# Two-piece weight splitting and a parametric rectifier, each with fewer operations

## The chip, the cores and the metric

The kernel runs on one core of a Trainium2 chip. Its engines are TensorE (PE for matmuls, PEld for the loads of their stationary operands), VectorE (DVE), ScalarE (ACT), GpSimd (POOL) and SyncE (SP), which issues transfers. The metric is the device time of one execution in microseconds, lower is better. The time before is the median of three runs, 837.42 us (836.5 to 838.45).

## The reference

The first half is attention inside chunks of 64 positions, for 8 batches, 8 heads, 576 positions and a head size of 64. Its result, laid out as 4608 tokens of 512 features, goes through a two-layer network with a parametric rectifier between the layers:

```python
scores = scale * np.matmul(q_c, k_c.transpose(0, 1, 2, 4, 3))
scores = scores - np.max(scores, axis=-1, keepdims=True)
attn = np.exp(scores)
attn = attn / (np.sum(attn, axis=-1, keepdims=True) + 1e-09)
out = np.matmul(attn, v_c)
...
h = x @ w_in                                   # 4608x512 by 512x2048
g = np.maximum(h, 0.0) + alpha * np.minimum(h, 0.0)
return (g @ w_out).astype(np.float32)          # 4608x2048 by 2048x512
```

The weights w_in and w_out arrive as 64-bit floats, all else as 32-bit floats. alpha has one value for each of the 2048 hidden features.

## The kernel before

**Precision.** TensorE runs the network's matmuls on the type fp32r. Every operand is held as two pieces, a rounded high piece and the rest, and each product is made of three passes: high by high, high by low, low by high.

**Splitting the weights.** The weights come as 32 raw tiles of 128x512 64-bit words (16 of w_in, 16 of w_out; 512 KB each), fetched by SP into a ring of three buffers (`raw` twice, `more` once). `split_weight` (lines 118 to 139) turns one raw tile into a high and a low piece by integer operations on the two 32-bit words of each float. ACT takes the absolute value (L130) and later copies the high piece with rounding (L134). DVE does the rest: limits of the exponent (L131), shift (L132), sign (L133), the low mantissa bits out of both words (L135, L136), the bare power of two (L137) and the product that is the low piece (L138). The tile `t1` carries the high part, `t3` the low bits.

**The rectifier.** `prelu` (L303 to L306) is called with a 128x512 block h in PSUM (or, in places, in SBUF), features on partitions. ACT makes relu(-h) (L304), ACT multiplies it by alpha per partition (L305), and DVE computes max(h, 0) minus that (L306). Then ACT rounds g to its high piece (L326) and DVE subtracts it for the low one (L327).

**Stages.** The first 1536 tokens (three blocks of 512) go through the network plainly: 48 steps, each of 12 matmuls for one slice of 128 hidden features (L314), the rectifier, and 12 matmuls into four PSUM accumulators (L339). The other 3072 tokens go in three pairs of blocks, by a product with seven block multiplications instead of eight (first layer L626, second layer L759), whose weight combinations are made ahead: `combine` adds and splits quarters of the weights (L523 to L540) in steps 20 to 43, and POOL stores them to memory (L501).

**Attention beside it.** Attention comes in 36 pieces of 128 tokens. The first eight run with scores (L180), maximum and its scaling (DVE L210, L212), eight exponentials (ACT L217), normalization (DVE L219 to L221), transposition on TensorE (L245), copies into a block-diagonal tile (ACT L252, L253), values (L263) and the split of x (ACT L295, DVE L296). The first four of these must be done before the first matmul of the network. The other 28 are "visits" between the steps: scores (L194), softmax, a DVE transposition (L228), eight small transfers (L235, tile `pT`), and values one visit later (L275), whose result ACT copies out (L291, L300; DVE L301).

**The order.** A scheduler with a model of the engines writes the order of each engine's instructions. Calls under `tc.high_priority` are moved forward. From step 20 on, TensorE's order is held to the order in the source (`pinned`); before that the scheduler is free with TensorE too. Each engine then runs its list strictly in order, so an instruction that waits holds back all behind it.

The per-partition factors alpha are fetched by a POOL transfer (L450) after POOL's memsets.

Of the kernel before, what the change touches and what calls it, by code (L numbers as in the profile page):

```python
# [9 lines left out]
F32 = mybir.dt.float32  # L10
F32R = mybir.dt.float32r
AF = mybir.ActivationFunctionType
ALU = mybir.AluOpType
AX = mybir.AxisListType
U32 = mybir.dt.uint32
# [3 lines left out]
def bits(pattern):  # L19
    return struct.unpack("f", struct.pack("I", pattern))[0]  # L20
# [7 lines left out]
def tile_local_attention_prelu_ffn(  # L28
# [12 lines left out]
    nc = tc.nc  # L41
    P = 128
# [5 lines left out]
    NF = w_in.shape[1]  # L48
# [13 lines left out]
    const = ctx.enter_context(tc.tile_pool(name="const", bufs=1))  # L62
# [4 lines left out]
    stage = ctx.enter_context(tc.tile_pool(name="stage", bufs=2))  # L67
# [5 lines left out]
    def f32(t):  # L73
        return t.bitcast(F32)
# [24 lines left out]
    ident = const.tile([P, P], F32, name="ident")  # L99
    make_identity(nc, ident)  # L100
    alpha_sb = const.tile([P, NF], F32, name="alpha_sb")

    pinned = [False]

# [9 lines left out]
    def fetch(side, f):  # L114
        name = ("raw", "raw", "more")[fetched[0] % 3]
        fetched[0] += 1
        raws[side, f] = stage.tile([P, 512], I64, name=name, bufs=2 if name == "raw" else 1)
        nc.sync.dma_start(out=raws[side, f], in_=(w_in if side == "wi" else w_out)[:, f])

    def split_weight(side, f):  # L120
        if (side, f) not in raws:
            fetch(side, f)
        raw = raws.pop((side, f))
        words = raw.bitcast(U32).rearrange("p (n two) -> p two n", two=2)
        low, high = words[:, 0], words[:, 1]
        t1 = stage.tile([P, 512], U32, name="t1")
        t3 = stage.tile([P, 512], U32, name="t3", bufs=1)
        w = const.tile([P, 2, 512], F32R, name=f"{side}{f}")
        hi, lo = w[:, 0], w[:, 1]
        nc.scalar.activation(f32(t1), f32(high), AF.Abs)  # L130
        nc.vector.tensor_scalar(f32(t1), f32(t1), bits(0x38000000), bits(0x47EFFFFF), op0=ALU.max, op1=ALU.min)  # L131
        nc.vector.tensor_scalar(t1, t1, 3, 0x3FFFF000, op0=ALU.logical_shift_left, op1=ALU.bitwise_and)  # L132
        nc.vector.scalar_tensor_tensor(t1, in0=high, scalar=0xC0000000, in1=t1, op0=ALU.bitwise_and, op1=ALU.bitwise_or)  # L133
        nc.scalar.copy(hi, f32(t1))  # L134
        nc.vector.tensor_scalar(t3, high, 0x1FF, 15, op0=ALU.bitwise_and, op1=ALU.logical_shift_left)  # L135
        nc.vector.scalar_tensor_tensor(t3, in0=low, scalar=17, in1=t3, op0=ALU.logical_shift_right, op1=ALU.bitwise_or)  # L136
        nc.vector.tensor_scalar(t1, t1, 0xFF800000, None, op0=ALU.bitwise_and)  # L137
        nc.vector.scalar_tensor_tensor(lo, in0=t3, scalar=2.0 ** -35, in1=f32(t1), op0=ALU.mult, op1=ALU.mult)  # L138
        return w

    def prepare(f, behind=None):
        with tc.issue_after(behind.ins) if behind else nullcontext():
            wi[f] = split_weight("wi", f)
            wo[f] = split_weight("wo", f)
# [157 lines left out]

    def prelu(g, h, f):  # L303
        nc.scalar.activation(g, h, AF.Relu, scale=-1.0)  # L304
        nc.scalar.activation(g, g, AF.Copy, scale=alpha_sb[:, f:f + 1])  # L305
        nc.vector.scalar_tensor_tensor(g, in0=h, scalar=0.0, in1=g, op0=ALU.max, op1=ALU.subtract)  # L306

    def ffn_in(x, f):
        xh, xl = x
        hps = ps_h.tile([P, TB], F32, name="ps_h")  # L310
        passes = [(0, xh), (0, xl), (1, xh)]
        for i, (l, xx) in enumerate(passes):
            for k in range(NK):
                pe(nc.tensor.matmul(  # L314
                    hps,
                    lhsT=wi[f][:, l, k * P:(k + 1) * P],
                    rhs=xx[:, k],
                    start=(i == 0 and k == 0),
                    stop=(i == 2 and k == NK - 1),
                ))  # L320
        g = gp.tile([P, TB], F32, name="g")
        gh = gp.tile([P, TB], F32R, name="gh")
        gl = gp.tile([P, TB], F32R, name="gl")
        with tc.high_priority(offset=HIGH):
            prelu(g, hps, f)
            nc.scalar.copy(gh, g)  # L326
            low = nc.vector.tensor_tensor(gl, g, f32(gh), op=ALU.subtract)  # L327
        stages["split"] = stages.get("split", [])[-1:] + [low]
        return gh, gl
# [118 lines left out]
    first_v(2)  # L448
    fetch("wi", 1)
    nc.gpsimd.dma_start(out=alpha_sb, in_=alpha)  # L450
    prepare(0)
    ready = 1
    for i in range(SPB + 2):
# [177 lines left out]
    def first_product(ops, g, j):  # L631
# [20 lines left out]
        with tc.high_priority(offset=HIGH):  # L652
            prelu(g[JF + j][:, 1], t, JF + j)
        for ps, i, f, col in ((c, 3, j, 1), (d, 4, JF + j, 0)):
            part(ps, i, False)
            with tc.high_priority(offset=HIGH):
                h = gp.tile([P, TB], F32, name="gl")
                nc.vector.tensor_tensor(h, ps, u, op=ALU.add)
                prelu(g[f][:, col], h, f)
# [199 lines left out]
    for pair in range(NPAIR):  # L859
# [4 lines left out]
        g = {}  # L864
# [49 lines left out]
```

## Time and profile before

| What | Value |
| --- | --- |
| Median of three runs | 837.42 us (836.5 to 838.45) |
| Span of the profiled execution, first to last instruction | 833.9 us |
| The runs above that span | 2.6 to 4.6 us, the median 3.5 us |
| PE busy | 804.0 us (96%) |
| DVE busy | 669.6 us (80%) |
| ACT busy | 548.0 us (66%) |
| Start of the first network matmul | 36.76 us |

The profile gives the profiled execution its span and no other time; the time of a run also holds what lies before the first and after the last instruction. In the lists, "idle before" is how long an engine stood still ahead of an instruction, with the one that released it behind the arrow. A matmul's shown duration is longer than the distance between two matmuls in a row, since they are pipelined.

### The profile page before, as it was taken

What the parts mean: (1) busy time and instruction counts of PE and PEld (TensorE: products, weight loads), DVE (VectorE), ACT (ScalarE), POOL (GpSimd) and SP (SyncE); (2) the same over time, 40 slices, a digit from 0 to 9 for tenths busy, and PEclk for the clock granted to TensorE, in tenths of its full rate; (3) what the DMA queues carried; (4) which work ended last, traced back from release to release, by engine and by line L of the source; (5) the groups of instructions that cost most, each with busy time, mean ns of one, the idle gap of its engine ahead of it and who ended that gap; (6) DMA issues with size and microseconds to landing.
All of it is one profiled execution on the core that took longest, in us unless ns stands there. A gap on an engine that the chain in (4) does not pass through costs nothing.

```text
span 833.9 us, 15382 instructions
## 1 busy us (share of the span) xinstructions
PE 804.0 (96%) x5248; PEld 642.6 (77%) x5248; DVE 669.6 (80%) x1240; ACT 548.0 (66%) x1420; POOL 215.4 (26%) x340
## 2 busy tenths in 40 slices
PE   4799999999999999999999999999999999999998
PEld 3577888777777778778778787787887888888886
DVE  6899999987788886677779996777789965668875
ACT  5986676657666776677886555777665546566452
POOL 4006223224244431111112242111122412121232
PEclk9999999999999999999999999999999999999999
DMA  9629778657698768688876799886557995555788
GB/s 287 206 77 344 236 243 266 199 162 209 200 254 216 247 211 262 214 258 270 263 240 209 225 252 329 256 274 199 192 196 242 244 300 184 188 191 187 235 230 231
DMA packets 73966, 192.40 MB, mean 231 GB/s; under 512 B 11664, under 2 KB 19104, under 8 KB 73760
## 3 DMA queue, kind: packets, MB, share of 16 engines
q0 software_dynamic: 38272, 127.43, 49.1%
q1 hardware_dynamic: 27248, 48.91, 18.5%
q10 hardware_dynamic: 8368, 15.08, 5.7%
q8 instruction: 42, 0.69, 0.3%
q14 instruction: 36, 0.29, 0.1%
HBM read 135.27 MB, written 42.99 MB: 214 GB/s over the span
## 4 chain that ended last, share of the span: by engine, by line
PE 73%; DVE 8%; DMA 7%; ACT 6%; SPq 3%; issue 3%; ACTq 0%; DVEq 0%; POOL 0%
PE ps_o L626 17%; PE ps_o L759 14%; PE ps_h L759 12%; PE ps_h L314 9%; PE ps_o L339 9%; PE ps_h L626 8%; SPq L235 3%; DMA v_sb<-v 2%; DMA pT<-t 2%; PE ps_a L275 1%; ACT pr L217 1%; DMA wi<-kT 1%; PE ps_a L194 1%; ACT wo L217 1%; DVE gl L327 1%
## 5 line engine op out<-in xcount | busy, mean ns | idle before, releaser
L339 PE MATMUL ps_o<-wo,gh 128*128 128x512 f32 x384 | 114.5, 396 | 0.6 <-ACT more L369 0.6
L314 PE MATMUL ps_h<-xh,wi 128*128 128x512 f32 x384 | 107.0, 401 | 1.8 <-DVE g L306 1.7
L314 PEld LDWEIGHTS ps_h<-xh,wi 128*128 128x128 f32 x384 | 71.8, 190 | 20.1 <-DVE g L306 2.6
L339 PEld LDWEIGHTS ps_o<-wo,gh 128*128 128x128 f32 x384 | 71.6, 188 | 18.1 <-ACT more L369 1.0
L339 PE MATMUL ps_o<-wo,gl 128*128 128x512 f32 x192 | 69.3, 396 | 0.4 <-DVE gl L327 0.4
L626 PE MATMUL ps_o<-wi,raw 128*128 128x512 f32 x171 | 67.9, 397 | 0.0
L217 ACT ACTIVATE pr<-ps_a,mx 128x64 f32<-128x64 f32 x224 | 67.4, 327 | 0.6
L626 PE MATMUL ps_o<-wo,raw 128*128 128x512 f32 x171 | 67.8, 396 | 0.0
L314 PE MATMUL ps_h<-xl,wi 128*128 128x512 f32 x192 | 52.6, 395 | 0.0
L326 ACT CAST gh<-g 128x512 fp32r<-128x512 f32 x48 | 29.8, 621 | 29.3 <-DVE g L306 27.4
L217 ACT ACTIVATION_READ_ACCUMULATOR pr<-ps_a,mx 128x1 f32 x224 | 48.9, 218 | 0.0
L564 POOL DMA_DIRECT2D raw<-wi_a x42 | 22.4, 535 | 102.1 <-PE ps_o L626 61.7
L304 ACT ACTIVATE wo<-gh 128x512 f32<-128x512 f32 x24 | 15.2, 634 | 51.1 <-DVE gh L649 51.1
L582 ACT CAST gh<-wi 128x512 fp32r<-128x512 f32 x45 | 28.0, 623 | 25.2 <-PE ps_o L759 10.9
L564 POOL DMA_DIRECT2D raw<-wo_a x42 | 22.4, 534 | 84.7 <-PE ps_o L759 43.9
L339 PEld LDWEIGHTS ps_o<-wo,gl 128*128 128x128 f32 x192 | 35.9, 188 | 9.6 <-DVE gl L327 0.8
L314 PEld LDWEIGHTS ps_h<-xl,wi 128*128 128x128 f32 x192 | 36.0, 188 | 8.5
L304 ACT ACTIVATE g<-ps_h 128x512 f32<-128x512 f32 x48 | 29.3, 611 | 18.3 <-PE ps_h L314 16.9
L626 PE MATMUL ps_o<-wi,wo 128*128 128x512 f32 x99 | 39.3, 397 | 0.0
L626 PE MATMUL ps_o<-wo,wo 128*128 128x512 f32 x99 | 39.1, 395 | 0.0
L626 PEld LDWEIGHTS ps_o<-wo,raw 128*128 128x128 f32 x171 | 32.2, 188 | 7.7
L626 PEld LDWEIGHTS ps_o<-wi,raw 128*128 128x128 f32 x171 | 32.1, 188 | 7.6
(252 smaller groups left out, 2280.9 us busy)
## 6 DMA issues: line engine op xcount, KB each, us to landing
raw<-wi_a POOLq DMA_DIRECT2D x42, 512.0 KB, 4.8
raw<-wo_a POOLq DMA_DIRECT2D x42, 512.0 KB, 4.1
wi<-wi_a POOLq DMA_DIRECT2D x21, 512.0 KB, 4.5
wo<-wi_a POOLq DMA_DIRECT2D x21, 512.0 KB, 4.8
wi<-wo_a POOLq DMA_DIRECT2D x21, 512.0 KB, 3.8
wo<-wo_a POOLq DMA_DIRECT2D x21, 512.0 KB, 4.3
v_sb<-v SPq DMA_DIRECT2D x28, 256.0 KB, 4.5
pT<-t SPq DMA_DIRECT2D x224, 32.0 KB, 3.9
```

The source lines that it names most:

```text
L194: pe(nc.tensor.matmul(att[par][c * C:(c + 1) * C, (NP + hp) * C:(NP + hp + 1) * C], lhsT=q_sb[rows, 2 * hp + c], rhs=kb[rows, 2 * hp + c], ...
L217: last = nc.scalar.activation(pr[:, g], one, AF.Exp, bias=mx[:, g], scale=SCALE, accum_out=sm[:, g])
L235: nc.sync.dma_start(out=pT[dst, i].rearrange("p h t -> p (h t)"), in_=tb[src, j].rearrange("p h t -> p (h t)"),)
L275: pe(nc.tensor.matmul(att[c][par * C:(par + 1) * C, hp * C:(hp + 1) * C], lhsT=v_sb[rows, h * C:(h + 1) * C], rhs=p[rows, :, par * NP + hp ...
L304: nc.scalar.activation(g, h, AF.Relu, scale=-1.0)
L314: pe(nc.tensor.matmul(hps, lhsT=wi[f][:, l, k * P:(k + 1) * P], rhs=xx[:, k], start=(i == 0 and k == 0), stop=(i == 2 and k == NK - 1),))
L326: nc.scalar.copy(gh, g)
L339: pe(nc.tensor.matmul(o, lhsT=a[:, ts], rhs=wo[f][:, l], start=(f == first and i == 0), stop=(f == last and i == 2),))
L564: streamed[0] = nc.gpsimd.dma_start(out=f32(t), in_=units[side][n])
L582: hi = nc.scalar.copy(t_hi, t)
L626: pe(nc.tensor.matmul(ps, lhsT=w[:, l, k * P:(k + 1) * P], rhs=xx[:, xl], start=first and at == 0, stop=at == n - 1, skip_group_check=not ...
L759: pe(nc.tensor.matmul(ps[m], lhsT=w[:, l, m * P:(m + 1) * P], rhs=xx, start=i != 6 and j == 0 and n == 0, stop=j == JF - 1 and n == 2, ski ...
```

## The change

The diff has two parts.

In `split_weight` the first word's mantissa is no longer cut after 11 bits: with the top three bits of the low word put behind it, `t1` becomes one 32-bit float with the weight's 24 leading bits. ACT rounds it to the high piece as before, and DVE subtracts the high piece from it for the low one. The three operations on `t3`, the mask and the multiplication go; one shift-and-or and one subtraction come. The low piece holds what 24 bits leave of the weight, where it held more bits before.

In `prelu` the sum is written as h + (1 - alpha) * relu(-h). A tile `rise` holds 1 - alpha, made once by DVE after alpha has come. ACT's multiplication by alpha goes; DVE's one operation multiplies by `rise` per partition and adds h.

```diff
@@ -99,6 +99,7 @@
     alpha_sb = const.tile([P, NF], F32, name="alpha_sb")
+    rise = const.tile([P, NF], F32, name="rise")
@@ -124,18 +125,15 @@
         t1 = stage.tile([P, 512], U32, name="t1")
-        t3 = stage.tile([P, 512], U32, name="t3", bufs=1)
         w = const.tile([P, 2, 512], F32R, name=f"{side}{f}")
         hi, lo = w[:, 0], w[:, 1]
         nc.scalar.activation(f32(t1), f32(high), AF.Abs)
         nc.vector.tensor_scalar(f32(t1), f32(t1), bits(0x38000000), bits(0x47EFFFFF), op0=ALU.max, op1=ALU.min)
-        nc.vector.tensor_scalar(t1, t1, 3, 0x3FFFF000, op0=ALU.logical_shift_left, op1=ALU.bitwise_and)
+        nc.vector.tensor_scalar(t1, t1, 3, 0x3FFFFFF8, op0=ALU.logical_shift_left, op1=ALU.bitwise_and)
         nc.vector.scalar_tensor_tensor(t1, in0=high, scalar=0xC0000000, in1=t1, op0=ALU.bitwise_and, op1=ALU.bitwise_or)
+        nc.vector.scalar_tensor_tensor(t1, in0=low, scalar=29, in1=t1, op0=ALU.logical_shift_right, op1=ALU.bitwise_or)
         nc.scalar.copy(hi, f32(t1))
-        nc.vector.tensor_scalar(t3, high, 0x1FF, 15, op0=ALU.bitwise_and, op1=ALU.logical_shift_left)
-        nc.vector.scalar_tensor_tensor(t3, in0=low, scalar=17, in1=t3, op0=ALU.logical_shift_right, op1=ALU.bitwise_or)
-        nc.vector.tensor_scalar(t1, t1, 0xFF800000, None, op0=ALU.bitwise_and)
-        nc.vector.scalar_tensor_tensor(lo, in0=t3, scalar=2.0 ** -35, in1=f32(t1), op0=ALU.mult, op1=ALU.mult)
+        nc.vector.tensor_tensor(lo, f32(t1), f32(hi), op=ALU.subtract)
         return w
@@ -302,8 +300,7 @@
     def prelu(g, h, f):
         nc.scalar.activation(g, h, AF.Relu, scale=-1.0)
-        nc.scalar.activation(g, g, AF.Copy, scale=alpha_sb[:, f:f + 1])
-        nc.vector.scalar_tensor_tensor(g, in0=h, scalar=0.0, in1=g, op0=ALU.max, op1=ALU.subtract)
+        nc.vector.scalar_tensor_tensor(g, in0=g, scalar=rise[:, f:f + 1], in1=h, op0=ALU.mult, op1=ALU.add)
@@ -448,6 +445,7 @@
     nc.gpsimd.dma_start(out=alpha_sb, in_=alpha)
+    nc.vector.tensor_scalar(rise, alpha_sb, -1.0, 1.0, op0=ALU.mult, op1=ALU.add)
     prepare(0)
```

The scheduler writes new orders from this. Line numbers below the two functions shift by 2 or 3 in the changed kernel: the new bits are L134, the subtraction L136, `rise` L448, the rectifier L302 and L303, g's rounding L323.

**DVE, the opening.** Names: `mx` and `sm` are a softmax's maximum and sum, `wo_94` the probabilities of the first two attention pieces. Before, from the first piece's maximum to its normalization:

```order
L210 TENSOR_REDUCE mx<-ps_a 128x8
L212 TENSOR_SCALAR mx<-mx 128x8
L137 TENSOR_SCALAR t_147<-t_147 128x512
L138 SCALAR_TENSOR_TENSOR wi_149<-t_148,t_147 128x512
L210 TENSOR_REDUCE mx<-ps_a 128x8
L219 TENSOR_SCALAR sm<-sm 128x8
L212 TENSOR_SCALAR mx<-mx 128x8
L220 RECIPROCAL sm<-sm 128x8
L221 TENSOR_TENSOR wo_94<-wo_94,sm 128x512
```

and in the changed kernel:

```order
L208 TENSOR_REDUCE mx<-ps_a 128x8
L134 SCALAR_TENSOR_TENSOR t_149<-raw,t_149 128x512
L210 TENSOR_SCALAR mx<-mx 128x8
L136 TENSOR_TENSOR wi_150<-t_149,wi_150 128x512
L208 TENSOR_REDUCE mx<-ps_a 128x8
L210 TENSOR_SCALAR mx<-mx 128x8
L217 TENSOR_SCALAR sm<-sm 128x8
L448 TENSOR_SCALAR rise<-alpha_sb 128x16
L218 RECIPROCAL sm<-sm 128x8
L219 TENSOR_TENSOR wo_94<-wo_94,sm 128x512
L208 TENSOR_REDUCE mx<-ps_a 128x8
```

`rise`, which waits for alpha, stands ahead of the first piece's reciprocal and normalization and of the third piece's maximum.

**PE, ahead of the network's first matmuls.** L180 are scores, L245 transpositions, L263 values of an attention piece, L314 the network (in the changed kernel L178, L243, L261, L311). Before:

```order
L180 MATMUL ps_a<-wo_86,wi_93 64x128 x8
L245 MATMUL ps_o_431<-ident,wo_94 128x128 x4
L263 MATMUL ps_o_334<-wi_91,wi_97 64x128 x8
L263 MATMUL ps_o_462<-wo_88,wo_96 64x128 x8
L314 MATMUL ps_h<-xh,wi_149 128x512 x4
L314 MATMUL ps_h<-xh,wi_506 128x512 x4
L245 MATMUL ps_o_473<-ident,wo_94 128x128 x4
L314 MATMUL ps_h<-xl,wi_149 128x512 x4
```

and in the changed kernel:

```order
L261 MATMUL ps_o_330<-wi_91,wi_97 64x128 x8
L178 MATMUL ps_a<-wo_86,wi_93 64x128 x8
L243 MATMUL ps_o_427<-ident,wo_94 128x128 x4
L311 MATMUL ps_h<-xh,wi_150 128x512 x4
L311 MATMUL ps_h<-xh,wi_501 128x512 x4
L243 MATMUL ps_o_469<-ident,wo_94 128x128 x4
L261 MATMUL ps_o_458<-wo_88,wo_96 64x128 x8
L311 MATMUL ps_h<-xl,wi_150 128x512 x4
```

The values of the fifth piece (on `wo_88`) stood ahead of the network's first matmuls and now stand behind the first eight of them.

**ACT, one visit in the stage of the weight combinations.** L217 are exponentials, L291 the copy that frees the PSUM tile, L539 the rounding of a weight combination. Before:

```order
L217 ACTIVATE pr,sm<-ps_a,mx 128x64 x4
L304 ACTIVATE g<-ps_h 128x512
L217 ACTIVATE pr,sm<-ps_a,mx 128x64 x4
L291 COPY xh<-ps_a 128x4x64 x2
L539 CAST raw<-t_3016 128x512
L305 ACTIVATE g<-g,alpha_sb 128x512
L539 CAST raw<-t_3018 128x512
L304 ACTIVATE g<-ps_h 128x512
L326 CAST gh<-g 128x512
L305 ACTIVATE g<-g,alpha_sb 128x512
L326 CAST gh<-g 128x512
```

and in the changed kernel:

```order
L215 ACTIVATE pr,sm<-ps_a,mx 128x64 x3
L302 ACTIVATE g<-ps_h 128x512
L215 ACTIVATE pr,sm<-ps_a,mx 128x64 x5
L289 COPY xh<-ps_a 128x4x64 x2
L537 CAST raw<-t_2887 128x512
L537 CAST raw<-t_2889 128x512
L323 CAST gh<-g 128x512
L302 ACTIVATE g<-ps_h 128x512
L323 CAST gh<-g 128x512
```

Two multiplications by alpha per visit are gone, and the rest keeps its sequence but for the place of a rounding.

## The prediction

> **What bounds the kernel now.** I read the page's first part, then the busy time by stretches, then who waited for whom on TensorE, and last the opening in order of time.
>
> ```profile
> span 833.9 us, 15382 instructions
> PE 804.0 (96%) x5248; PEld 642.6 (77%) x5248; DVE 669.6 (80%) x1240; ACT 548.0 (66%) x1420; POOL 215.4 (26%) x340
> core 0: us, PE busy (x) PEld busy (x) DVE busy (x) ACT busy (x) POOL busy (x), PEclk, DMA share, GB/s
> 30.00:40.00 10.00, 7.13 (x58) 5.44 (x55) 7.44 (x18) 9.93 (x42) 0.00 (x0) 0.83 0.38 116
> 40.00:160.00 120.00, 118.81 (x584) 94.53 (x583) 115.00 (x237) 79.36 (x148) 34.17 (x44) 1.00 0.70 228
> 160.00:200.00 40.00, 40.00 (x318) 31.84 (x317) 37.10 (x78) 28.22 (x97) 13.31 (x18) 1.00 0.58 182
> 200.00:340.00 140.00, 133.46 (x1146) 105.39 (x1145) 114.71 (x232) 94.70 (x307) 46.16 (x62) 1.00 0.75 222
> 340.00:834.00 494.00, 489.44 (x2983) 393.03 (x2981) 374.29 (x627) 314.29 (x733) 112.67 (x195) 1.00 0.75 236
> ```
>
> TensorE sets the end. After 40 us it is idle for 1.2 us up to 160, none up to 200, 6.5 us up to 340, and 4.6 us after that, nearly all of it the tail behind the last matmul. DVE is busy for 115 of 120 us between 40 and 160, yet TensorE hardly waits there: DVE is full, not late. So what the change takes off DVE and ACT pays only where TensorE waits for them. The waits of TensorE after 40 us (total us, times, longest):
>
> ```profile
> PE ps_a L275 <- ACT xh L291: 2.0, 2, 1.2
> PE ps_h L314 <- DVE g L306: 1.7, 2, 1.2
> PE ps_a L275 <- ACT xl L291: 1.0, 1, 1.0
> PE ps_a L275 <- DMA pT<-t: 1.0, 1, 1.0
> PE ps_a L194 <- DMA k_sb<-kT: 0.6, 1, 0.6
> PE ps_o L339 <- ACT more L369: 0.6, 1, 0.6
> PE ps_a L275 <- DVE xl L301: 0.5, 1, 0.5
> PE ps_o L339 <- DVE gl L327: 0.4, 1, 0.4
> PE ps_o L759 <- DVE gl L583: 0.2, 1, 0.2
> ```
>
> They sum to 8.0 us in 11 waits. Each costs more than it shows, because a matmul is shown longer than its turn:
>
> ```profile
> L339 PE MATMUL ps_o<-wo,gh 128*128 128x512 f32 x384 | 114.5, 396 | 0.6 <-ACT more L369 0.6
> 356.56 2.80 PE ps_o L626 x12
> 36.76 3.04 PE ps_h L314 x8
> ```
>
> 396 ns shown, 2.80/12 = 233 ns per turn (the second row is from the chain), so a wait loses another 0.16 us, and all 11 together 9.8 us. That is the whole prize after the opening. In the opening up to 40 us TensorE is busy for 22 us; there ACT is full (9.93 of 10 us in the window from 30 to 40) with softmax work that the change does not touch.
>
> **The change part by part.** The prices:
>
> ```profile
> L135 DVE TENSOR_SCALAR t<-raw 128x512 uint32<-128x512 uint32 x22 | 9.6, 436 | 3.4 <-DMA raw<-w_in 3.4
> L136 DVE SCALAR_TENSOR_TENSOR t<-raw,t 128x512 uint32<-128x512 uint32 x22 | 15.0, 682 | 0.1
> L137 DVE TENSOR_SCALAR t<-t 128x512 uint32<-128x512 uint32 x32 | 13.9, 436 | 0.6 <-ACT wi L134 0.4
> L138 DVE SCALAR_TENSOR_TENSOR wi<-t,t 128x512 fp32r<-128x512 uint32 x16 | 10.9, 681 | 0.1
> L327 DVE TENSOR_TENSOR gl<-g,gh 128x512 fp32r<-128x512 f32 x48 | 32.8, 683 | 5.4 <-ACT gh L326 5.1
> L305 ACT ACTIVATE g<-g,alpha_sb 128x512 f32<-128x512 f32 x48 | 35.6, 742 | 0.6
> L305 ACT ACTIVATE wo<-wo,alpha_sb 128x512 f32<-128x512 f32 x48 | 34.1, 709 | 0.0
> L305 ACT ACTIVATE wi<-wi,alpha_sb 128x512 f32<-128x512 f32 x48 | 33.2, 713 | 0.0
> L306 DVE SCALAR_TENSOR_TENSOR g<-ps_h,g 128x512 f32<-128x512 f32 x48 | 32.6, 679 | 1.8 <-ACT g L305 1.8
> L304 ACT ACTIVATE g<-ps_h 128x512 f32<-128x512 f32 x48 | 29.3, 611 | 18.3 <-PE ps_h L314 16.9
> ```
>
> *Weights.* Per raw tile 436 + 682 + 436 + 681 = 2235 ns of DVE go; a shift-and-or (682, L136's form) and a subtraction into fp32r (683, L327's form) come: 870 ns less, 28 us over 32 tiles. ACT's part and the fetches stay. The high piece is ready 0.68 us later, since the new bits go in ahead of the rounding; nobody waits for that, as the first network matmul is at 36.76 us and later tiles have each predecessor 0.87 us shorter. All of the 28 us lies under TensorE's full stretch from 40 to 200 us, so directly it is worth nothing. Were a tile to come late, its 0.68 us would show; I bound that at one such wait, in the term for new waits below.
>
> *Rectifier.* ACT loses 144 operations, 35.6 + 34.1 + 33.2 = 103 us in all, and each chain from h to g's high piece is 0.71 to 0.74 us shorter. DVE's operation keeps its form but takes its factor from a tile. No row shows that on DVE. The nearest is ACT, where L305 with a factor from a tile takes 742 against 611 for L304 with a constant (though that reads PSUM); so 0 to +131 ns. I take 0, as the form and sizes of L306 stay. At the upper bound DVE would get 19 us more, two thirds of it after 340 us, where it is busy 374 of 494 us, and the chain is still 0.6 us shorter.
>
> *What that gives, wait by wait.* Each figure has the 0.16 us added per wait. (a) The rectifier's own waits (L314 on L306 twice, L339 on L327 once): 2.0 + 0.6 = 2.6 us; two have an L305 in their chain and DVE queues in front, I take 2.0, bounds 0 and 2.6. (b) Waits for ACT's copies (L291 three times, L369 once): 3.5 + 0.7 = 4.2 us.
>
> ```profile
> 279.50 0.73 ACT L305 ACTIVATE g<-g,alpha_sb 128x512 f32<-128x512 f32 x1
> 281.70 0.21 ACT L214 ACTIVATE mx<-mx 128x8 f32<-128x8 f32 x1 [1.48 <-DVE mx L210]
> 284.80 0.68 ACT L291 COPY xl<-ps_a 128x256 f32<-128x256 f32 x2
> ...
> L138 DVE SCALAR_TENSOR_TENSOR wo<-t,t x16: 673/678/690, 24.2 to 171.6; 128x512 fp32r<-128x512 uint32 x16
> ```
>
> The first three rows are the last of the L291 waits. The copy stands behind eight exponentials, these behind a scaled maximum that waited 1.48 us for DVE's maximum. So ACT's freed 0.73 us is not what is late there, DVE's queue is; and that queue is relieved because the weight splits, whose last operation (last row: first and last start) began at 171.6 us, end earlier and the combinations move forward. I take half, 2.2, bounds 0 and 4.2. (c) L301 behind DVE: 0.7, bounds 0 and 0.7. (d) The two waits for transfers, 1.9 us, and the pairs' 0.4 us: 0, bounds 0 and 2.3, since a shorter softmax issues `pT` earlier only if SP is free.
>
> *New waits.* Before step 20 the scheduler has rewritten TensorE's order, and DVE's and ACT's everywhere. TensorE had lost 1.2 us between 40 and 200 us, so there is little to win and something to lose; I take +0.8 us, half the longest wait that shows above plus its 0.16, bounds 0 and 3.
>
> *The opening.* `rise` waits for alpha:
>
> ```profile
> L450 POOL DMA_DIRECT2D alpha_sb<-alpha x1: 686/686/686, 9.2 to 9.2; - x1
> DMA to landing us min/median/max: 5.5/5.5/5.5
> 13.29 0.16 DVE L219 TENSOR_SCALAR sm<-sm 128x8 f32<-128x8 f32 x1
> 13.72 0.69 DVE L221 TENSOR_TENSOR wo<-wo,sm 128x512 f32<-128x512 f32 x1
> 16.57 0.59 ACT L252 COPY wo<-ps_o 64x512 f32<-64x512 f32 x1
> 35.01 1.64 PE L263 MATMUL ps_o<-wo,wo 128*64 128x128 f32 x16 [1.86 <-DVE t L136]
> ```
>
> Alpha lands at 9.2 + 5.5 = 14.7 us, and `rise` stands right behind L219 at 13.4 us, so DVE stands for about 1.3 us with the first normalization behind it. ACT needs that result at 16.57 us. Normalization from 15.1 to 15.8, four transpositions of 0.8 us: 16.7, so ACT, the full engine, loses 0.15. Up to the cast that starts the network, ACT's new list has one weight rounding more (+0.62) and one pair of copies fewer (-1.17), so L314 starts about 0.4 us earlier. But the fifth piece's values, which ran in idle time at 35.01, now stand behind the first eight network matmuls; undisturbed such a group takes 1.09 us, now of TensorE's full time. Sum +0.7 us; bounds -0.5 (the group still hidden) and +2.0 (the 1.3 us wait passes through whole).
>
> The eight matmuls at 36.76 took 3.04 us instead of 1.9, and the window from 30 to 40 has a granted clock of 0.83: an idle TensorE starts slow. The Trainium skill (TensorE: Matmul & The Clock Gate, Part 1: The HAM clock gate) says the array runs at half rate after an idle window of about 3.4 us and until a busy one has passed; the trace agrees, as 0.83 over 10 us is 3.4 us at half rate. By that rule an order that closes or opens an idle stretch here moves the time by another 1.2 us.
>
> *Sum.* -2.0 - 2.2 - 0.7 + 0.8 + 0.7 = -3.4 us on 833.9: a span of 830.5. The runs' median lies 3.5 us above the span, so 834.0 us.
>
> **The rivals.** *More goes:* all of (a), (b), (c) and half of (d), with no new waits: -2.6 - 4.2 - 0.7 - 1.2 + 0.7 = -8.0, 829.4 us. For it: 115 us of DVE in 120 become about 92 (26 of the 32 tiles at 0.87), and the combinations get a head start. Against: each list is in order, so what stands at the wrong place stays late. *Nothing measurable:* only the rectifier's waits go and the opening's and new waits' costs eat them: -2.0 + 0.8 + 1.0 = -0.2, 837.2 us. For it: TensorE at 96%, and transfers in the chain of 200 to 340. *Slower, by the opening:* alpha's transfer lands later than DVE's place for `rise`, and the delay goes through: first normalization, first transposition, ACT's copies, which are the full engine's; +1.3, the displaced group +1.1, a slow stretch of matmuls +1.2, and only (a) regained: +1.6 to +3.6, 840 us. It decides once the first L314 (new L311) starts after 38 us. Against: ACT needs the result 0.1 us before it would come. *The clock:* the half-rate stretch ahead of L314 doubles while all else goes as forecast: 835.2; by the row at 36.76, 1.2 us. *The change does not do what it says:* a subtraction or the tile factor slower than priced; at the upper bound of 131 ns nothing moves TensorE, so it falls in with "nothing measurable".
>
> **How the numbers follow.** Forecast 0.38 (832 to 836); more goes 0.22; clock 0.04; nothing measurable 0.20; slower 0.16. A change under 0.2%, 1.7 us, can't be told from none here: faster is below 835.7. Faster 0.38 + 0.22 + 0.04 = 0.64, same 0.20, slower 0.16. The forecast's own bounds are 833.9 - 9.8 - 0.5 + 3.5 = 827.1 and, with new waits at 3, the opening at 2.0 and nothing regained, 842.4; neither end is likely. The range 828.5 to 839.5 takes in the large gain and half of the slower case.
>
> **What would show it.** In the changed profile: DVE about 640 us busy (669.6 - 28), ACT about 445; the 40-to-160 stretch's DVE near 92 us; waits on L303, the new rectifier, gone from TensorE's list, and those on L289 (old L291) halved; DVE idle ahead of `rise` for about 1.3 us; first L311 between 36 and 37.5 us; PE's idle time in 200 to 340 at 3 to 5 us. It is wrong if TensorE shows new waits of more than 2 us between 40 and 200, if ACT is idle in the opening for more than 1 us, or if the waits between 200 and 340 keep their sum with DVE idle, which would mean that transfers, not DVE and ACT, hold the visits.

## The result, and the profile after

The changed kernel takes 833.99 us (median of 12 runs, 831.71 to 835.83), the kernel before on the same chip 837.36 us (12 runs, 836.5 to 841.79). The ratio is 0.9948 with a 95% interval of 0.9932 to 0.9964: faster by half a per cent, and the forecast was 834.0.

The page's first part and the stretches used for the kernel before (busy time of each engine, with the number of instructions):

```profile
span 832.4 us, 15117 instructions
PE 805.4 (97%) x5248; PEld 644.8 (77%) x5248; DVE 656.0 (79%) x1177; ACT 465.8 (56%) x1276; POOL 212.4 (26%) x340
...
30.00:40.00 10.00, 6.45 (x70) 5.23 (x72) 7.12 (x17) 9.52 (x37) 0.00 (x0) 1.00 0.51 177
40.00:160.00 120.00, 118.31 (x568) 93.75 (x566) 106.96 (x199) 69.50 (x141) 35.40 (x49) 1.00 0.73 239
160.00:200.00 40.00, 40.00 (x347) 31.87 (x346) 33.63 (x69) 24.43 (x84) 15.40 (x21) 1.00 0.61 193
200.00:340.00 140.00, 136.20 (x1159) 108.40 (x1157) 111.23 (x222) 81.45 (x291) 40.30 (x54) 0.99 0.71 210
340.00:833.00 493.00, 487.95 (x2977) 392.46 (x2976) 378.40 (x627) 260.44 (x636) 112.27 (x195) 1.00 0.77 236
```

TensorE's idle time between 200 and 340 us fell from 6.5 to 3.8 us; between 40 and 160 it rose from 1.2 to 1.7. DVE lost 13.6 us and ACT 82. The waits of TensorE after 40 us, all of them (us in total, times, longest):

```profile
PE ps_a L273 <- DMA pT<-t: 2.7, 2, 2.4
PE ps_a L261 <- ACT wi L251: 1.3, 1, 1.3
PE ps_a L273 <- ACT xl L289: 1.1, 2, 0.6
PE ps_o L757 <- DVE gl L581: 0.3, 2, 0.2
PE ps_h L311 <- DVE g L303: 0.3, 1, 0.3
```

8.0 us in 11 waits became 5.7 in 8. The rectifier's waits went from 2.1 to 0.3 us, those for ACT's copies of a visit (L289, before L291) from 3.6 with the one for L369 to 1.1, and the one for L301 is gone. The transfers' rose from 1.6 to 2.7, and the one for the copy L251, at 60 us, is new. The groups of DVE that the change touches:

```profile
L303 DVE SCALAR_TENSOR_TENSOR g<-g,rise,ps_h 128x512 f32<-128x512 f32 x48 | 35.6, 741 | 5.0 <-ACT g L302 5.0
L134 DVE SCALAR_TENSOR_TENSOR t<-raw,t 128x512 uint32<-128x512 uint32 x22 | 15.3, 695 | 0.2
L131 DVE TENSOR_SCALAR t<-t 128x512 f32<-128x512 f32 x32 | 13.6, 430 | 10.9 <-ACT t L130 10.9
L136 DVE TENSOR_TENSOR wi<-t,wi 128x512 fp32r<-128x512 f32 x16 | 11.0, 689 | 2.2 <-ACT wi L135 2.2
```

The new operations of the weights cost what was forecast (695 and 689 ns); the rectifier's with its factor from a tile costs 741 against 679. And DVE now stands for 10.9 us ahead of L131 (3.2 before), the head of a weight tile, waiting for ACT's absolute value. The opening, in order of time:

```profile
14.98 0.17 DVE L448 TENSOR_SCALAR rise<-alpha_sb 128x16 f32<-128x16 f32 x1 [1.18 <-DMA alpha_sb<-alpha]
...
37.20 2.12 PE L311 MATMUL ps_h<-xh,wi 128*128 128x512 f32 x8 [2.29 <-ACT xh L293]
39.69 1.09 PE L261 MATMUL ps_o<-wo,wo 128*64 128x128 f32 x16
...
58.49 0.60 ACT L302 ACTIVATE g<-ps_h 128x512 f32<-128x512 f32 x1 [2.58 <-PE ps_h L311]
60.20 1.09 PE L261 MATMUL ps_a<-wi,wi 128*64 128x128 f32 x16 [1.30 <-ACT wi L251]
```

`rise` stands 1.18 us for alpha, the first network matmul starts 0.44 us later than before, and the fifth piece's values follow the first eight. At 58.49 ACT waits 2.58 us for TensorE's own matmul, with the copies L250 and L251 behind it in its list, and TensorE then waits for those.

The trace also gives the start of each 128x512 matmul of TensorE, called a wide matmul here. How much later each comes than in the kernel before shows where time was lost and won, here and in the runs below:

| profiled execution | 1st (36.76 us before) | 201st (92.89) | 641st (199.57) | 1001st (303.58) | 3161st (827.80) |
| --- | --- | --- | --- | --- | --- |
| changed kernel | +0.44 | +1.75 | +1.76 | -1.26 | -1.55 |
| e1, weights only | +1.38 | +5.18 | +5.19 | +2.80 | +4.72 |
| e2, rectifier only | +0.07 | +0.54 | +0.45 | -1.49 | -2.49 |
| e3, `rise` by GpSimd | -0.38 | +3.27 | +3.28 | -0.12 | -0.23 |
| e4, first two slices old | -0.15 | +2.77 | +2.81 | -0.64 | -0.85 |
| e11, first eight slices old | +0.53 | +1.93 | +1.81 | -1.46 | -2.43 |
| e12, ACT's load back | +0.65 | +5.35 | +5.26 | -0.32 | -1.51 |

The change loses 1.75 us before 95 us, holds that loss to 200, and wins 3.0 between 200 and 303. One execution is only good to a few us: that of before lies some 1.7 us under its median (see the offset, below), and the 70 runs of the kernel before that stood beside all these lie between 834.8 and 841.8 us.

### The profile page after: what moved, and what is told of

Same layout as the page of the kernel before. It is cut to its first block, busy times and chain, and to the rows that moved or that the text cites. A ratio compares the mean times of both kernels' runs of the same rounds, so it can differ in the third digit from the quotient of the medians.

```text
span 832.4 us, 15117 instructions
## 1 busy us (share of the span) xinstructions
PE 805.4 (97%) x5248; PEld 644.8 (77%) x5248; DVE 656.0 (79%) x1177; ACT 465.8 (56%) x1276; POOL 212.4 (26%) x340
## 4 chain that ended last, share of the span: by engine, by line
PE 84%; DMA 6%; ACT 4%; DVE 4%; issue 1%; SPq 1%; POOL 0%; DVEq 0%; ACTq 0%
PE ps_o L624 19%; PE ps_o L757 15%; PE ps_o L336 12%; PE ps_h L311 12%; PE ps_h L757 12%; PE ps_h L624 9%; PE ps_a L273 2%; PE ps_a L192 1%; DMA raw<-w_in 1%; DMA pT<-t 1%; DMA wi<-qT 1%; DMA more<-w_in 1%; DMA wo_a<-raw 1%; ACT pr L215 1%; SPq L233 1%
## 5 line engine op out<-in xcount | busy, mean ns | idle before, releaser
L336 PE MATMUL ps_o<-wo,gh 128*128 128x512 f32 x384 | 116.4, 396 | 0.1
L311 PE MATMUL ps_h<-xh,wi 128*128 128x512 f32 x384 | 106.1, 400 | 2.6 <-ACT xh L293 2.3
L311 PEld LDWEIGHTS ps_h<-xh,wi 128*128 128x128 f32 x384 | 71.6, 189 | 20.3 <-ACT xh L293 2.5
L336 PE MATMUL ps_o<-wo,gl 128*128 128x512 f32 x192 | 71.2, 396 | 0.0
L311 PE MATMUL ps_h<-xl,wi 128*128 128x512 f32 x192 | 53.1, 397 | 0.0
L302 ACT ACTIVATE wo<-gh 128x512 f32<-128x512 f32 x24 | 15.2, 633 | 52.0 <-DVE gh L647 52.0
L323 ACT CAST gh<-g 128x512 fp32r<-128x512 f32 x48 | 29.9, 624 | 24.1 <-DVE g L303 15.2
L311 PEld LDWEIGHTS ps_h<-xl,wi 128*128 128x128 f32 x192 | 36.3, 190 | 8.9 <-issue 0.2
L324 DVE TENSOR_TENSOR gl<-g,gh 128x512 fp32r<-128x512 f32 x48 | 32.8, 684 | 8.8 <-ACT gh L323 8.5
L302 ACT ACTIVATE g<-ps_h 128x512 f32<-128x512 f32 x48 | 29.2, 608 | 18.8 <-PE ps_h L311 18.7
L303 DVE SCALAR_TENSOR_TENSOR g<-g,rise,ps_h 128x512 f32<-128x512 f32 x48 | 35.6, 741 | 5.0 <-ACT g L302 5.0
```

Of the source, the lines that this page charges most:

```text
L303: nc.vector.scalar_tensor_tensor(g, in0=g, scalar=rise[:, f:f + 1], in1=h, op0=ALU.mult, op1=ALU.add)
L311: pe(nc.tensor.matmul(hps, lhsT=wi[f][:, l, k * P:(k + 1) * P], rhs=xx[:, k], start=(i == 0 and k == 0), stop=(i == 2 and k == NK - 1),))
L336: pe(nc.tensor.matmul(o, lhsT=a[:, ts], rhs=wo[f][:, l], start=(f == first and i == 0), stop=(f == last and i == 2),))
```

## The experiments

**The parts apart, and two guesses on the opening.** e1 is the kernel before with the new `split_weight` alone, e2 with the new `prelu` and `rise` alone. e3 and e4 are the whole change with one edit each:

```diff
-    nc.vector.tensor_scalar(rise, alpha_sb, -1.0, 1.0, op0=ALU.mult, op1=ALU.add)
+    nc.gpsimd.tensor_scalar(rise, alpha_sb, -1.0, 1.0, op0=ALU.mult, op1=ALU.add)
```

```diff
-            wi[f] = split_weight("wi", f)
-            wo[f] = split_weight("wo", f)
+            split = split_weight_old if f < 2 else split_weight
+            wi[f] = split("wi", f)
+            wo[f] = split("wo", f)
```

> The weight part alone, the old rectifier kept. Theory (the opening's loss comes with the weight part, which puts the fifth piece's values behind the network's first eight matmuls; the gain between 200 and 340 us comes from both parts): TensorE's 40th network matmul 1.5 to 2.5 us later than in the kernel before, as in the whole change (51.4 before, 53.6 after), DVE about 28 us less busy, a regain of 1 to 2 us between 200 and 340; time 836 to 838 us, ratio 0.998 to 1.001. Rival A (the weights carry the gain, since DVE's queue was late): 833 to 835, ratio 0.995 to 0.997. Rival B (the opening's loss comes from the wait for alpha, which this kernel does not have): 40th matmul within 0.5 us of before.

> The rectifier alone, the old weight splitting kept; the opening's order on TensorE is that of the kernel before, and the operation that waits for alpha is there. Theory: no loss in the opening (40th network matmul within 0.5 us of 51.4), ACT 103 us less busy, the rectifier's waits gone and part of the visits': 833 to 835 us, ratio 0.994 to 0.997. Rival A (DVE's queue was late, so only the weights help): 836 to 838, ratio 0.998 to 1.001. Rival B (the wait for alpha costs the opening): 40th matmul 1 to 2 us later than before.

> The whole change, but 1 - alpha is made by GpSimd, so that DVE does not stand for alpha; TensorE's order is the changed kernel's row by row. Theory (ACT, not DVE, is full in the opening and needs the first normalization only 0.1 us before it comes): first network matmul at 36.9 to 37.3 us against 37.20, time equal to the changed kernel's, ratio 0.993 to 0.997. Rival (the wait of 1.2 us goes through): first network matmul at 36.0 to 36.3, time 1 us less, ratio 0.992 to 0.994.

> The whole change, but the first two slices' four weight tiles are split the old way, which brings back TensorE's order of the opening of the kernel before (the fifth piece's values ahead of the network's first matmuls). Theory: the opening's loss of 1.7 us goes, so 40th network matmul within 0.7 us of 51.4, and the rest keeps its gain: 831 to 833 us, ratio 0.991 to 0.994. Rival (the loss is the later high piece or DVE's wait for alpha, not the order): 40th matmul again 2 us late, 833.5 to 835, ratio 0.995 to 0.997.

| run | us, median of 12 | range | ratio to before, 95% |
| --- | --- | --- | --- |
| e1 | 840.49 | 838.62 to 844.32 | 1.0041, 1.0024 to 1.0058 |
| e2 | 834.44 | 833.12 to 838.10 | 0.9973, 0.9957 to 0.9990 |
| e3 | 835.89 | 833.17 to 837.73 | 0.9978, 0.9962 to 0.9995 |
| e4 | 834.71 | 832.42 to 836.66 | 0.9971, 0.9956 to 0.9986 |

The rectifier alone can hardly be told from the whole: the two intervals just overlap. The weights alone, which take 20 us off DVE (649.6 us busy), make the kernel 0.4% slower, outside all that was expected of e1, and in the profile they lose it by the 201st wide matmul (+5.18). The parts don't add: -3.0 and +3.1 us apart make nothing, together they make -3.4. The scheduler writes another order for each kernel. e3 starts the network's first matmul 0.82 us earlier than the whole change does, so `rise`'s wait does pass through to it. But its first eight wide matmuls then take 3.23 us, at a granted clock of 0.63 between 36 and 40 us, where the changed kernel's take 2.12 at 1.00, and it is no faster at the end, which neither side expected. e4 puts the fifth piece's values back ahead of the first network matmuls; the opening loss stays (+2.77 at the 201st), so that group isn't the cause, or not alone. Some of e4's loss is clock too: 0.50 between 36 and 40 us, against 0.65 before.

**TensorE's order held.** In the runs above the scheduler also rewrites TensorE's order. So four kernels were run with that order held to the source from the network's first step; between kernels with and without the weight part it then differs in one swapped pair of groups alone.

```diff
-        pinned[0] = n >= 20
+        pinned[0] = n >= 0
```

> The kernel before with TensorE held to the source's order from the first step of the network on, not from step 20. It is the base of the next three, in which TensorE's order is the same row by row (but for one transposition and one group of values that change places in the opening where the weight part is in). Theory and rival say the same of it: the source's order is not made for this, 838 to 846 us, ratio 1.001 to 1.010.

> The weight part alone under the held order. Theory (the weight part lost 3 us in the run before because the scheduler wrote another order for TensorE in the first 70 us, not by its own operations): 0 to 2.5 us faster than the held kernel before, by the regain between 200 and 340 us. Rival (its own operations lose: the high piece 0.68 us later, the rounding in ACT's list waiting for it): 2 us or more slower than the held kernel before.

> The rectifier alone under the held order. Theory (ACT's 103 us and the shorter chain carry the gain): 2 to 4 us faster than the held kernel before. Rival (the gain of the rectifier was the luck of an order): within 1 us of it.

> The whole change under the held order. Theory (the parts add where the order is the same): faster than the held kernel before by the sum of the two single gains, 2 to 6 us, and not slower than the rectifier alone. Rival (the weight part costs by its operations): 1 us or more slower than the rectifier alone under the held order.

All four are slower than the free order, by far more than was expected (some 25 us for e5, where 1 to 8 were): e5 starts its first network matmul 16 us later. But they can be compared with each other: before 861.51 us (6 runs, 858.83 to 866.69), weights 867.20 (5, 866.33 to 870.08), rectifier 855.93 (4, 855.70 to 858.36), both 862.05 (5, 860.00 to 865.48). As ratios to the free kernel before: 1.0306 (1.0278 to 1.0334), 1.0375 (1.0354 to 1.0396), 1.0238 (1.0217 to 1.0259), 1.0297 (1.0277 to 1.0317). The rectifier is worth 5.6 to 5.2 us (2 to 4 were expected), the weight part costs 5.7 to 6.1, though TensorE does the same in the same order. So the theory that the loss is TensorE's order falls; it comes from the other engines. (The traces of e5 and e8 are of executions 5.2 and 3.4 us above their medians, so they are compared below place by place and not by their ends.) Theory three, after the prediction's own and that of the order, was that the weight tile's new chain is at fault: all of it hangs on ACT's absolute value, where before `t3` needed the raw tile alone, so DVE stands wherever ACT is late (the 10.9 us ahead of L131).

**The theory of ACT's late first operation.** e9 is e8 with the first four slices split in the old way (`f < 4`). e10 is e8 with the absolute value made by DVE for every tile:

```diff
-        nc.scalar.activation(f32(t1), f32(high), AF.Abs)
+        nc.vector.tensor_scalar(t1, high, 0x7FFFFFFF, None, op0=ALU.bitwise_and)
```

> The whole change, but the first four slices' eight weight tiles are split in the old way; TensorE's order held to the source, and equal to that of the run with the rectifier alone held (855.9 us; with both parts held 862.1). Theory three: the new splitting loses only in the opening, because its whole chain hangs on ScalarE's absolute value and ScalarE is late there, so VectorE's list stands. Then 854 to 858 us, the first network matmul at 51 to 52.5 us (55.3 with both parts), and VectorE's idle time ahead of the weight limits within the first 60 us under 2 us. Rival: the new splitting loses wherever it stands, or through the order of the later lists: 860 to 864 us.

> The whole change, TensorE's order held, but the absolute value of each weight tile is made by VectorE (one bitwise AND of 0.44 us) in place of ScalarE, so that the chain's head needs the raw tile alone; VectorE gets 14 us more, ScalarE about 19 us less. If the wait of the chain's head on ScalarE is what costs (theory three): 855 to 859 us, and the waits of the weight limits on ScalarE (9.3 us in 5 times) gone. Rival: the tail of the chain costs (the new bits ahead of the rounding, the subtraction behind it) or VectorE's load does: 860 to 864 us.

e9 takes 858.53 us (6 runs, 856.06 to 862.21; ratio 1.0268, 1.0244 to 1.0292), between rectifier and both; its profiled execution, 856.06, runs the same span as e7's. The median is just outside the 854 to 858 of theory three, and the first network matmul came at 49.05, earlier than the 51 to 52.5 expected. The first four slices hold some half of the loss by the medians, and the interval can't say it closer. e10 takes 860.82 us (6 runs, 857.88 to 863.40; ratio 1.0286, 1.0264 to 1.0308), no better than e8 within the interval. Its waits on ACT's absolute value are gone from DVE's list, 9.3 us before 100 us in e8, and in their place stand waits for the raw tiles themselves:

```profile
DVE t L130 <- DMA more<-w_out: 4.2, 1, 4.2
DVE t L130 <- DMA raw<-w_in: 2.8, 1, 2.8
...
DVE t L130 <- DMA raw<-w_out: 1.6, 3, 1.0
```

So that theory falls as it was put: the wait ahead of L131 was real, and taking it away brought nothing that could be measured. (e10 also gives DVE the work of the absolute values, so what the wait alone costs isn't shown.) What does cost is seen by putting the same place of e7 and e8 side by side, in order of time. TensorE's last transposition ahead of the network waits for a normalized softmax (L222 in e7, L219 in e8). First e7, the rectifier alone:

```profile
44.60 0.17 DVE L213 TENSOR_SCALAR mx<-mx 128x8 f32<-128x8 f32 x1
47.40 0.17 DVE L220 TENSOR_SCALAR sm<-sm 128x8 f32<-128x8 f32 x1 [2.63 <-ACT wo L218]
47.60 0.20 DVE L221 RECIPROCAL sm<-sm 128x8 f32<-128x8 f32 x1
47.84 0.69 DVE L222 TENSOR_TENSOR wo<-wo,sm 128x512 f32<-128x512 f32 x1
48.45 0.68 DVE L297 TENSOR_TENSOR xl<-ps_o,xh 128x512 fp32r<-128x512 f32 x1
49.05 0.42 DVE L132 TENSOR_SCALAR t<-t 128x512 f32<-128x512 f32 x1
49.38 0.42 DVE L136 TENSOR_SCALAR t<-raw 128x512 uint32<-128x512 uint32 x1
49.72 0.42 DVE L132 TENSOR_SCALAR t<-t 128x512 f32<-128x512 f32 x1
...
48.68 1.08 PE L246 MATMUL ps_o<-ident,wo 128*128 128x128 f32 x4 [3.65 <-DVE wo L222]
```

Then e8, with the new splitting:

```profile
45.61 0.17 DVE L210 TENSOR_SCALAR mx<-mx 128x8 f32<-128x8 f32 x1
48.27 0.69 DVE L294 TENSOR_TENSOR xl<-ps_o,xh 128x512 fp32r<-128x512 f32 x1 [2.49 <-ACT xh L293]
48.88 0.76 DVE L131 TENSOR_SCALAR t<-t 128x512 f32<-128x512 f32 x2
49.55 0.17 DVE L217 TENSOR_SCALAR sm<-sm 128x8 f32<-128x8 f32 x1
49.62 0.76 DVE L132 TENSOR_SCALAR t<-t 128x512 uint32<-128x512 uint32 x2
50.29 0.20 DVE L218 RECIPROCAL sm<-sm 128x8 f32<-128x8 f32 x1
50.40 0.64 DVE L133 SCALAR_TENSOR_TENSOR t<-raw,t 128x512 uint32<-128x512 uint32 x1
50.96 0.69 DVE L133 SCALAR_TENSOR_TENSOR t<-more,t 128x512 uint32<-128x512 uint32 x1
51.56 0.69 DVE L219 TENSOR_TENSOR wo<-wo,sm 128x512 f32<-128x512 f32 x1
...
52.39 1.09 PE L243 MATMUL ps_o<-ident,wo 128*128 128x128 f32 x4 [6.47 <-DVE wo L219]
```

In e7 the normalization comes first and the weight tiles behind it. In e8 the scheduler has put the split of x and six weight operations of two tiles ahead of it, with the sum and its reciprocal in between. From the scaled maximum to the normalization it is 47.84 - 44.60 = 3.24 us in e7 and 51.56 - 45.61 = 5.95 in e8: 2.7 us, and TensorE's wait grows by 2.8 (3.65 to 6.47). About 0.5 of the 2.7 is ACT's: in e8 the rounding of x (L293) stands ahead of the last two exponentials. The other 2.2 are DVE's list. e10, with the bitwise AND in it, has six lighter operations of the two tiles at that place:

```profile
50.54 1.09 PE L243 MATMUL ps_o<-ident,wo 128*128 128x128 f32 x4 [5.33 <-DVE wo L219]
```

The six profiles with TensorE's order held fall into two groups by this place:

| run | splitting of the first slices | normalization behind the weight tiles | scaled maximum to normalization | TensorE's wait there | first network matmul | median |
| --- | --- | --- | --- | --- | --- | --- |
| e5 | old | no | 3.24 | 3.45 | 53.02 | 861.5 |
| e7 | old | no | 3.24 | 3.65 | 51.60 | 855.9 |
| e9 | old | no | 3.23 | 3.41 | 49.05 | 858.5 |
| e6 | new | yes | 5.95 | 5.85 | 55.01 | 867.2 |
| e8 | new | yes | 5.95 | 6.47 | 55.31 | 862.1 |
| e10 | new, AND by DVE | yes | 5.44 | 5.33 | 53.47 | 860.8 |

So 2.7 us of the weight part's loss of some 6 arise at this place, most of them because the scheduler puts the weight tiles in DVE's list ahead of a softmax that TensorE waits for. Why it puts the shorter chain there is its own reckoning, and no trace shows it. No run moved these operations alone, and the rest of the 6 us wasn't followed to single waits; that e9 starts the network earliest without being the fastest shows that there is more.

The same thing happens in the free order, in e1. Its softmax of a later piece has its last exponential done at 56.7 us, and its reciprocal at 58.00. Between that and the normalization stands the low piece of a weight tile, which waits for ACT's rounding:

```profile
58.00 0.19 DVE L217 RECIPROCAL sm<-sm 128x8 f32<-128x8 f32 x1
59.64 0.69 DVE L135 TENSOR_TENSOR wi<-t,wi 128x512 fp32r<-128x512 f32 x1 [1.45 <-ACT wi L134]
60.25 0.68 DVE L218 TENSOR_TENSOR wi<-wi,sm 128x512 f32<-128x512 f32 x1
...
61.08 0.63 PE L242 MATMUL ps_a<-ident,wi 128*128 128x128 f32 x4 [1.68 <-DVE wi L218]
```

TensorE stands 1.68 us for it. The changed kernel has no such wait after 40 us (its waits are listed above), so its own opening loss isn't shown to come from there.

**Back in the free order: a mixture, and ACT's load.** e11 is the whole change with the first eight slices split in the old way (`f < 8`). e12 is the whole change with a multiplication on ACT behind each low piece, whose result nobody reads:

```diff
             low = nc.vector.tensor_tensor(gl, g, f32(gh), op=ALU.subtract)
+            nc.scalar.activation(g, g, AF.Copy, scale=alpha_sb[:, f:f + 1])
```

> The whole change with the scheduler free, but the first eight slices' sixteen tiles are split in the old way. Theory three: the opening then runs as with the rectifier alone (200th wide matmul 0.3 to 1.0 us later than before, 1.75 in the whole change), and the lighter splitting of the rest keeps what it brings between 200 and 340 us: 831.5 to 833.5 us. Rival: what the weight part brings later is only the scheduler's luck: 834 to 836 us.

> The whole change, and behind each of the 48 low pieces of the plain stage ScalarE multiplies g once more by alpha, where nobody reads it: ScalarE's 36 us are back, the chain from h to g stays short. If the gain came from ScalarE's freed time (term b, its copies): 835.5 to 837 us. If it came from the shorter chain (term a): 833.5 to 834.7 us.

e11 takes 833.71 us (6 runs, 832.42 to 834.93; ratio 0.9964, 0.9951 to 0.9977): neither the expected gain of a us nor its loss, and its opening (+1.93) isn't that of the rectifier alone (+0.54). No version was found that is measurably faster than the changed kernel.

e12 takes 833.55 us (7 runs, 832.07 to 835.61; ratio 0.9963, 0.9949 to 0.9976). ACT's 35.0 us are back in it:

```profile
L325 ACT ACTIVATE g<-g,alpha_sb 128x512 f32<-128x512 f32 x48 | 35.0, 730 | 20.3 <-DVE gl L324 19.5 <-DMA pT<-t 0.6
```

TensorE's waits after 40 us stay at 5.6 us, with one of 1.3 for ACT's copy of a visit, and 1.4 us in which its second layer (L337) waits for pieces of g. So ACT's freed time in the plain stage, taken by itself, is worth nothing that can be measured; the load may have cost in the opening (+5.35 at the 201st matmul, one execution), but it was made up between 200 and 303 us. That leaves the shorter chain from h to g as what the rectifier gains there. It is found by exclusion: the scheduler's order is another in e12 too.

## Why the prediction was right, and where its steps were not

**The sum and the offset.** The forecast was -3.4 us on the span, and the medians differ by 837.36 - 833.99 = 3.4. The two profiled executions differ by 1.5 (833.9 and 832.4). The offset was misread: the profiled execution of the change took 834.16 us with a span of 832.4, so 1.8 us lie outside the span, and in every other run of the record it is 1.7 to 1.9. By that, the 3.5 us of the forecast were 1.8 and another 1.7 by which the profiled execution of before lay under its median. A sum that was too large against that execution and an offset that was too large met at 834.0. That the forecast came out to a hundredth is luck: its terms, taken below between the two executions, miss by up to 1.5 us and come to -1.5 together. The medians bear out the size of the gain; this account bears out less of it.

**(a), the rectifier's waits: right.** 2.0 us were forecast, 1.8 of the 2.1 shown are gone, and e2, with the rectifier alone, has the same 0.3 left. In e12, whose chain is as short, 1.4 us of waits for g's pieces are back with ACT's load, so ACT's list had a part in them.

**(b), ACT's copies: direction and reason right, size low.** Half was forecast, some 70% went (3.6 to 1.1). That ACT's freed 0.73 us wasn't what those copies lacked is borne out by e12 (1.3), and by e1, where ACT keeps its load, DVE is relieved and 1.4 are left. e2, where DVE keeps the old splitting, still waits 2.3 us for them. **(c)** went, as forecast.

**(d), transfers: taken as 0, cost 1.1.** The wait for `pT` at 250 us is 2.39 us long, and a stretch at half clock follows it (last section). TensorE's idle time from 200 to 340 is 3.8 us, in the 3 to 5 forecast.

**The opening: its sum held by luck, and the step that failed is "new waits", with its +0.8.** `rise` idles 1.18 us (1.3 forecast), and the displaced group costs its 1.09. But the first network matmul, though within the 36 to 37.5 that were named, comes 0.44 us later than before, and the sum had it 0.4 earlier. "ACT, the full engine, loses 0.15" was too low: e3 starts 0.82 us earlier without that wait. What made up for it is the clock: the first eight wide matmuls take 2.12 us and not 3.04, at a granted clock of 1.00 between 30 and 40 us against 0.83. The clock rival had named the opposite. So at the 17th wide matmul, behind the displaced group, the loss is 42.68 - 41.94 = 0.74 us, against +0.7.

From there to the 201st matmul another 1.0 us was lost, though the (a) wait of 1.2 lies in that stretch and went. With +0.8 and that gain about -0.5 was due, so the term came to some 2.3 in place of 0.8. The wait of 1.30 behind L251 is the largest part of it. TensorE's idle time in the stretch grew by 0.5 us; the other 0.5 of the 1.0 stand in no wait of the trace, and their cause is open. The rival "slower, by the opening" named the place rightly, though its point of decision, 38 us, wasn't reached.

**The weights: "directly it is worth nothing" was too kind.** The part alone costs 3 us in the free order and 5.7 to 6.1 with TensorE's order held. The prediction asked whether a tile would come late; it didn't ask what would stand behind the tile's operations in DVE's list. In the whole change the loss is smaller, and the part pays some back between 200 and 340 us: e1 wins 2.4 us on the kernel before from the 641st to the 1001st matmul (5.19 to 2.80), one execution each.

**DVE's and ACT's busy time: both off.** About 640 and 445 us were forecast, 656.0 and 465.8 came, and the stretch from 40 to 160 holds 107 us of DVE rather than 92. Two errors. The factor from a tile was taken at 0 and measured 741 - 679 = 62 ns, at most 9 us over 144, inside the bounds of 0 and 131. And operations were priced by their shown durations, but on DVE they overlap: in e7's rows an operation of 0.42 starts 0.33 us before the next, one of 0.68 starts 0.60 before. A tile thus frees two of 0.33 and two of 0.60 and gains two of 0.60: 0.66 us, 21 over 32 tiles. With the 9 that makes about 12 less, and 13.6 were measured (-20.0 in e1 and +6.1 in e2). ACT likewise gave 82 us for 144 operations, 0.57 each and not 0.72. No run ties the time to these sums.

## What to carry to other kernels

Where one engine sets the end, ask of every edit what stands behind its instructions in each in-order list, not how much busy time it removes: here 20 us less of DVE made the kernel slower by itself, and 35 us more of ACT off the chain cost nothing that could be measured. A shorter chain between two matmuls pays where TensorE waits at its end. Price an operation in a full list by the distance to the next start, not by its shown duration, and take the offset between span and run from the same execution. Before a loss of a us near a wait is put down to an order, look at the granted clock there.

## What the runs showed of the hardware

A short wait of TensorE cost more than itself. In the changed kernel the 2.39 us for `pT` were followed by 3.4 us at half clock, while the kernel before, whose waits there are no longer than 1.2 us, kept its clock in the same stretch. The stretches of the changed kernel and its first matmuls after the wait:

```profile
245.00:250.00 5.00, 2.92 (x14) 2.03 (x12) 1.73 (x4) 3.63 (x18) 0.84 (x1) 1.00 0.74 171
250.00:255.00 5.00, 4.68 (x71) 3.98 (x72) 4.25 (x9) 1.21 (x7) 0.00 (x0) 0.66 0.37 101
```

```profile
250.32 0.63 PE L273 MATMUL ps_a<-pT,v_sb 64*64 64x64 f32 x27 [2.39 <-DMA pT<-t]
...
251.84 2.07 PE L311 MATMUL ps_h<-xh,wi 128*128 128x512 f32 x4
253.71 1.32 PE L311 MATMUL ps_h<-xl,wi 128*128 128x512 f32 x4
254.88 1.11 PE L311 MATMUL ps_h<-xh,wi 128*128 128x512 f32 x4
```

Four matmuls took 2.07 us instead of 1.09, and a granted clock of 0.66 over 5 us is 3.4 us at half rate: 1.7 us lost behind the wait. The half clock doesn't begin with the wait but 0.5 us after it has ended: up to 250.5 us the granted clock is 1.00, and from 251 to 254 it is 0.50.

The wait alone doesn't decide it. The changed kernel, e3 and e12 all stand 2.3 us ahead of their first network matmul, in the same order of TensorE. Between 36 and 40 us the granted clock is then 1.00, 0.63 and 0.85, and the first eight wide matmuls take 2.12, 3.23 and 2.60 us.

The Trainium skill (TensorE: Matmul & The Clock Gate, Part 1: The HAM clock gate) puts half rate behind an idle window of about 3.4 us, full rate behind a busy one of that length, and lets the window run free of the kernel. The length of the slow stretch agrees with it, and so does the difference between the three kernels; the waits that went ahead are shorter, 2.3 and 2.39 us.

The clock isn't the whole of the spread of several us between runs of one kernel: of the 35 runs of the kernel before that stood beside e1, ten have the same mean granted clock, 0.996, and lie between 835.06 and 838.12 us.
